# Three activation tiles on the ScalarE queue and a reordered head, in an S5 + SwiGLU kernel

## The chip, the cores and the metric

One core of a Trainium2 chip runs the kernel. TensorE (PE) multiplies matrices and transposes, VectorE (DVE), ScalarE (ACT) and GpSimd (POOL) do the elementwise work, and SyncE (SP), ACT and POOL issue DMAs. The metric is the device time of one execution in microseconds, and of several executions the median.

## The reference

`x` is 2048 x 512 in bf16. It is layer-normalised without weights, and the result `xn` goes through two branches whose outputs are added to `x`:

```
xn = (x - mean) / sqrt(var + 1e-5)
A: Bu = xn @ B_bar^T (complex);  h_t = Lam_bar * h_{t-1} + Bu_t;  y = 2 Re(h @ C^T) + xn * Dskip
B: (silu(xn @ w_gate) * (xn @ w_up)) @ w_down          512 -> 1376 -> 512
out = x + A + B
```

## The kernel before

The 2048 rows are 16 tiles of 128 rows, in four chunks of four tiles (512 rows). For each chunk there are three kinds of matmul stage: gate and up (`gateup_tile`, line 427, 11 column tiles of 128), the B projection of the state space branch (`bproj_tile`, line 352), and the output (`out_ffn` line 514, `out_ssm` line 524). DVE runs the scans and rotations, ACT evicts PSUM. Instructions run on each engine in the order in which the program text issues them. DVE's longer work is put on a list (`queue`) and taken off it between matmul stages by estimated costs (`pump`, `need`); nothing of the change is on that list.

The change lies in the head, which makes the first chunk ready while the weights still arrive. What there is to know of it:

- **Loads** (lines 120 to 146). SP issues `x` tile 0, the two halves of gate's first column group (`load_w1_half`, line 118; a half is two of the four slices of 128 rows of the weight, 192 KB), `x` tile 2, the two halves of up's first group, `x` tile 3, then gate's and up's second group (line 113), the four `x` tiles of chunk 1 in one DMA (line 136), and the transposing loads of B (line 139). ACT issues `x` tile 1, then loads its function table (line 123). A tile of `x` is 128 KB.
- **Layernorm of one tile.** `ln_stats` (DVE, lines 183 and 184: statistics into `mv`), `ln_rstd_act` (ACT, lines 194 and 195: Ln and Exp give `rstd`), `norm_dve` (DVE, line 207: writes `xn`), `xT_pe` (PE, line 219: four 128 x 128 transposes into PSUM), and the copy of PSUM to `xnT` (ACT, line 223; for tile 3 DVE, line 221).
- **Matmuls** (`head_mm(i, groups, k0, k1)`, line 609): for tile `i` and the first three column tiles, a matmul of 128 x 128 x 128 for each slice k from k0 to k1. They need `xnT` of tile i and the weight's slices.
- **Dummy matmuls** (`dummy`, line 581) ahead of the first transpose, on a tile of zeros: ten of 512 columns, and three of 128 columns between the two halves of tile 0.

The order of the head is the text at lines 613 to 656:

```
dummy(10, CW)
... statistics, rstd and norm of tiles 0 and 1, transposes of tile 0
head_mm(0, wg_g, 0, HK)
xT_pe(1)
head_mm(0, wu_g, 0, HK)
ln_stats(2); ln_rstd_act(2)
head_mm(0, wg_g, HK, KD)
head_mm(0, wu_g, HK, KD)
ln_stats(3); norm_dve(2); ln_rstd_act(3)
head_mm(1, wg_g); xT_pe(2); norm_dve(3)
head_mm(1, wu_g); prm_transpose(); head_mm(2, wg_g)
xT_pe(3, on_dve=True); head_mm(2, wu_g)
```

After them come the matmuls of tile 3, the evictions of the held banks, and the steady stages.

Of the kernel before, what the change touches and what calls it, by code (L numbers as in the profile page):

```python
# [23 lines left out]
def kernel(  # L24
# [17 lines left out]
    nc = tc.nc  # L42
# [4 lines left out]
    CW = 512  # L47
# [3 lines left out]
    TPC = CW // 128  # L51
# [22 lines left out]
    def bank(shape=(128, CW), dtype=F32):  # L74
        return psum.tile(list(shape), dtype, name="ps")
# [4 lines left out]
    x_v = A_x[0].rearrange("(n p) d -> p n d", p=128)  # L80
# [5 lines left out]
    xall = const.tile([128, NT, D], BF16, name="xall")  # L86
# [3 lines left out]
    wg_g, wu_g = [], []  # L90
# [14 lines left out]
    def wslice(groups, fi, k):  # L105
        for (a, b), t in zip(fgroups, groups):
            if a <= fi < b:
                return t[:, k, (fi - a) * 128:(fi - a) * 128 + fsz[fi]]


    def load_w1(q, tiles, view, gi):
        a, b = fgroups[gi]
        q.dma_start(out=tiles[gi][:], in_=view[:, :, a * 128:min(F, b * 128)])


    def load_w1_half(tiles, view, gi, k0, k1):
        a, b = fgroups[gi]
        nc.sync.dma_start(out=tiles[gi][:, k0:k1, :], in_=view[:, k0:k1, a * 128:min(F, b * 128)])  # L118

    nc.sync.dma_start(out=xall[:, 0, :], in_=x_v[:, 0, :])  # L120
    nc.vector.memset(xall[:, 1, 0:2], 0.0)
    nc.scalar.dma_start(out=xall[:, 1, :], in_=x_v[:, 1, :])
    nc.scalar.preload_act_table_set("natural_log_exp_and_others")
    load_w1_half(wg_g, wg_v, 0, 0, KD // 2)
    load_w1_half(wg_g, wg_v, 0, KD // 2, KD)
    nc.sync.dma_start(out=xall[:, 2, :], in_=x_v[:, 2, :])  # L126
    load_w1_half(wu_g, wu_v, 0, 0, KD // 2)
    load_w1_half(wu_g, wu_v, 0, KD // 2, KD)
    nc.sync.dma_start(out=xall[:, 3, :], in_=x_v[:, 3, :])
    load_w1(nc.sync, wg_g, wg_v, 1)  # L130
    load_w1(nc.sync, wu_g, wu_v, 1)
    prm_rows = const.tile([128, 128], BF16, name="prm_rows")
# [44 lines left out]
    def xn_tile(c):  # L177
        if c not in xn_c:
            xn_c[c] = lnp.tile([128, TPC, D], BF16, name="xn")
        return xn_c[c]  # L180

    def ln_stats(n):
        nc.vector.bn_stats(out=stats[:, n, 0, :], in_=xall[:, n, :])  # L183
        nc.vector.bn_aggr(out=mv[:, n, :], in_=stats[:, n, 0, :])
# [8 lines left out]
    def ln_rstd_act(n):  # L193
        nc.scalar.activation(out=lnv[:, n:n + 1], in_=mv[:, n, 1:2], func=ACT.Ln, bias=eps_t[:])
        nc.scalar.activation(out=rstd[:, n:n + 1], in_=lnv[:, n:n + 1], func=ACT.Exp, scale=-0.5)
# [9 lines left out]
    def norm_dve(n, lo=0, hi=D):  # L205
        c, i = divmod(n, TPC)
        nc.vector.tensor_scalar(out=xn_tile(c)[:, i, lo:hi], in0=xall[:, n, lo:hi], scalar1=mv[:, n, 0:1],  # L207
                                scalar2=rstd[:, n:n + 1], op0=ALU.subtract, op1=ALU.mult)
# [6 lines left out]
    def xT_pe(n, k0=0, k1=KD, on_dve=False):  # L215
        c, i = divmod(n, TPC)
        tp = bank((128, KD, 128), BF16)
        for k in range(k0, k1):
            nc.tensor.transpose(out=tp[:, k, :], in_=xn_tile(c)[:, i, k * 128:(k + 1) * 128], identity=ident[:])  # L219
        if on_dve:  # L220
            nc.vector.tensor_copy(out=xnT[:, k0:k1, n * 128:(n + 1) * 128], in_=tp[:, k0:k1, :])
        else:
            nc.scalar.copy(out=xnT[:, k0:k1, n * 128:(n + 1) * 128], in_=tp[:, k0:k1, :])
# [355 lines left out]
    def dummy(n, cols):  # L579
        for _ in range(n):  # L580
            nc.tensor.matmul(warm[:, 0:cols], lhsT=junk[:, 0:128], rhs=junk[:, 0:cols], start=True, stop=True)
# [21 lines left out]
    def head_mm(i, groups, k0=0, k1=KD, tiles=range(H)):  # L603
        which = 0 if groups is wg_g else 1
        for fi in tiles:
            if len(held) <= fi:
                held.append((bank(), bank()))
            for k in range(k0, k1):
                nc.tensor.matmul(held[fi][which][:, i * 128:(i + 1) * 128], lhsT=wslice(groups, fi, k),  # L609
                                 rhs=xnT[:, k, i * 128:(i + 1) * 128], start=(k == 0), stop=(k == KD - 1))  # L610

    HK = KD // 2
    dummy(10, CW)
    ln_stats(0)
    ln_rstd_act(0)
    ln_stats(1)
# [6 lines left out]
    norm_dve(1)  # L623
    head_mm(0, wg_g, 0, HK)
    xT_pe(1)
    head_mm(0, wu_g, 0, HK)
    ln_stats(2)
    ln_rstd_act(2)
    head_mm(0, wg_g, HK, KD)
    head_mm(0, wu_g, HK, KD)  # L630
    ln_stats(3)
    norm_dve(2)
    ln_rstd_act(3)
    head_mm(1, wg_g)
    xT_pe(2)
# [148 lines left out]
```

## Time and profile before

| What | Value |
|---|---|
| median of 3 runs | 181.02 us (180.7 to 181.13) |
| the profiled execution's own time | 181.21 us |
| its span, first to last instruction | 179.4 us |
| mean granted TensorE clock | 0.999 |
| busy PE / DVE / ACT / POOL | 97% / 86% / 58% / 13% |
| DMA, mean over the span | 87 GB/s |
| the chain that ended last | PE 93%, DMA 2%, SP's issues 1%, DVE 1% |

The chain of waits is followed back from the last instruction to what released it. In the timeline, a row is start, duration, engine, line, operation, output and inputs; several like instructions are merged into one row with their count, and a bracket tells how long the engine had stood idle and what ended it. Times are microseconds from the span's start. PEld is TensorE's weight load, SPq and ACTq the issuing of DMAs. Matmuls are pipelined: a 128-column one is shown at about 0.22 us, while the next starts 0.06 us after it.

### The profile page before, as it was taken

The page shows a single profiled execution, that of the slowest core. Times are in us where ns is not written, and L with a number is a line of the kernel's source. Part 1 is how long each engine was busy: PE and PEld are TensorE (multiplying, and loading weights), DVE is VectorE, ACT ScalarE, POOL GpSimd, SP SyncE. Part 2 cuts the span into 40 slices and gives each one's busy share as a digit, 9 for nine tenths or more (in the row PEclk, how much of TensorE's full clock was granted, in tenths as well). Part 3 has the DMA queues.
Part 4 walks back from the last instruction along what each step waited for, and adds up shares of the span by engine and source line. Part 5 has one row for each costly group of instructions (what it writes and reads, how often), then busy time and mean ns, then how long its engine had stood idle before and what let it go on. Part 6 is the DMA issues. An engine that isn't in the chain of part 4 may idle for free.

```text
span 179.4 us, 2491 instructions
## 1 busy us (share of the span) xinstructions
PE 173.4 (97%) x908; PEld 83.4 (46%) x924; DVE 155.0 (86%) x248; ACT 104.8 (58%) x190; POOL 23.4 (13%) x30
## 2 busy tenths in 40 slices
PE   7899999999999999999999999999999999999993
PEld 2684444443444444444444444444444444444742
DVE  3649998799999999999999999999999986996033
ACT  3459956998299959022799661024866949805000
POOL 7001100000500000025400000014000004315000
PEclk9999999999999999999999999999999999999999
DMA  5999757994036600011840000007300007964512
GB/s 147 294 263 210 163 98 177 357 190 109 5 72 168 252 4 0 0 11 22 112 93 2 0 0 4 0 0 80 37 0 5 0 0 109 139 103 45 76 58 61
DMA packets 28492, 15.53 MB, mean 87 GB/s; under 512 B 18336, under 2 KB 28416, under 8 KB 28448
## 3 DMA queue, kind: packets, MB, share of 16 engines
q1 hardware_dynamic: 24592, 11.87, 28.5%
q0 software_dynamic: 3456, 3.28, 14.4%
q10 hardware_dynamic: 432, 0.23, 0.4%
q8 instruction: 7, 0.11, 0.3%
q14 instruction: 5, 0.04, 0.1%
HBM read 8.03 MB, written 5.24 MB: 74 GB/s over the span
## 4 chain that ended last, share of the span: by engine, by line
PE 93%; DMA 2%; SPq 1%; DVE 1%; issue 1%
PE ps L427 36%; PE ps L514 21%; PE ps L352 15%; PE ps L524 15%; DMA xall<-in_A_x_dram 2%; PE ps L609 2%; PE ps L453 2%; PE ps L463 1%; SPq L118 1%; DVE stats L183 0%; PE ps L219 0%; SPq L126 0%; SPq L120 0%; DVE xn L207 0%; DVE xall L527 0%
## 5 line engine op out<-in xcount | busy, mean ns | idle before, releaser
L514 PE MATMUL ps<-wd_sb,guT 128*128 128x512 bf16 (+4 forms) x195 | 38.6, 355 | 0.2
L427 PE MATMUL ps<-xnT,wg 128*128 128x512 bf16 x143 | 37.6, 379 | 0.3
L427 PE MATMUL ps<-xnT,wu 128*128 128x512 bf16 x146 | 37.5, 379 | 0.1
L394 DVE TENSOR_TENSOR_SCAN g<-r_t,car,u 128x512 bf16<-128x512 f32 x24 | 28.9, 1263 | 0.0
L524 PE MATMUL ps<-CF,wt 128*128 128x512 bf16 (+2 forms) x140 | 28.1, 355 | 0.2
L352 PE MATMUL ps<-xnT,BT 128*128 128x512 bf16 x126 | 28.2, 379 | 0.1
L514 PEld LDWEIGHTS <-guT 128*128 128x128 bf16 (+1 forms) x198 | 18.5, 98 | 19.9
L441 ACT ACTIVATE guT<-ps 128x512 bf16<-128x512 f32 x40 | 25.2, 629 | 2.5 <-PE ps L427 2.3
L442 ACT CAST u<-ps 128x512 bf16<-128x512 f32 x40 | 24.7, 618 | 2.7 <-PE ps L427 2.7
L427 PEld LDWEIGHTS <-wu 128*128 128x128 bf16 x148 | 14.5, 98 | 17.5
L427 PEld LDWEIGHTS <-wg 128*128 128x128 bf16 x148 | 14.3, 98 | 17.6 <-issue 0.8
L530 ACT CAST res<-ps 128x512 bf16<-128x512 f32 x12 | 6.8, 582 | 23.5 <-PE ps L524 23.5
L524 PEld LDWEIGHTS <-wt 128*128 128x128 bf16 x144 | 13.4, 98 | 14.3
L531 POOL DMA_DIRECT2D out_dram<-res x12 | 10.5, 1033 | 72.6 <-ACT res L530 67.5
L352 PEld LDWEIGHTS <-BT 128*128 128x128 bf16 x128 | 12.5, 98 | 15.1
L354 ACT CAST u<-ps 128x512 bf16<-128x512 f32 x32 | 17.7, 614 | 2.4 <-PE ps L352 2.2
L486 ACT ACTIVATE xr<-xall,nb,rstd 128x512 bf16<-128x512 bf16 x16 | 12.0, 808 | 8.4 <-DVE xall L492 5.9
L183 DVE BATCH_NORM_STATS2 stats<-xall 128x6 f32<-128x512 bf16 x16 | 10.7, 671 | 3.2 <-DMA xall<-in_A_x_dram 3.2
L446 DVE TENSOR_TENSOR guT<-guT,u 128x1024 bf16<-128x1024 bf16 x20 | 13.5, 679 | 0.0
L527 DVE TENSOR_TENSOR xall<-ps,xall 128x512 bf16<-128x512 f32 (+2 forms) x6 | 3.1, 514 | 9.1 <-PE ps L524 9.1
L199 POOL TENSOR_TENSOR rstd<-ve,neg_half 128x4 f32<-128x4 f32 x3 | 5.3, 1751 | 43.6 <-DVE ve L198 43.6
L362 DVE TENSOR_TENSOR pm<-u,c 128x2048 bf16<-128x2048 bf16 x8 | 9.8, 1221 | 1.2 <-ACT c L279 1.1
(101 smaller groups left out, 169.0 us busy)
## 6 DMA issues: line engine op xcount, KB each, us to landing
out_dram<-in_A_x_dram SPq DMA_DIRECT2D x1, 1536.0 KB, 8.7
out_dram<-res POOLq DMA_DIRECT2D x12, 128.0 KB, 3.2
out_dram<-xall POOLq DMA_DIRECT2D x3, 512.0 KB, 5.7
wd_sb<-in_B_w_down_dram SPq DMA_DIRECT2D x1, 1280.0 KB, 10.1
xall<-in_A_x_dram SPq DMA_DIRECT2D x1, 1024.0 KB, 5.9
wg<-in_B_w_gate_dram SPq DMA_DIRECT2D x1, 512.0 KB, 6.1
wu<-in_B_w_up_dram SPq DMA_DIRECT2D x1, 512.0 KB, 7.1
xall<-in_A_x_dram SPq DMA_DIRECT2D x1, 512.0 KB, 7.9
```

Of the source, the lines that this page charges most:

```text
L183: nc.vector.bn_stats(out=stats[:, n, 0, :], in_=xall[:, n, :])
L352: nc.tensor.matmul(ps[:], lhsT=BT[:, part, k, q * 128:(q + 1) * 128], rhs=xnT[:, k, c * CW:(c + 1) * CW], start=(k == 0), stop=(k == KD - 1))
L354: nc.scalar.copy(out=u_tiles[c][:, part, q, :], in_=ps[:])
L394: V.tensor_tensor_scan(out=g()[:, part, q, :], data0=r_t[:, q:q + 1].to_broadcast([128, CW]), data1=u_tiles[c][:, part, q, :], initial=ini ...
L427: nc.tensor.matmul(ps[:fs, lo:hi], lhsT=wslice(groups, fi, k), rhs=xnT[:, k, c * CW + lo:c * CW + hi], start=(k == 0), stop=(k == KD - 1))
L441: nc.scalar.activation(out=guT[:fs, fi, :], in_=psg[:fs], func=ACT.Silu)
L442: nc.scalar.copy(out=u_pair[c][:fs, fi % 2, :], in_=psu[:fs])
L446: products.append(lambda: V.tensor_tensor(out=g, in0=g, in1=u, op=ALU.mult))
L486: nc.scalar.activation(out=box["xr"][:], in_=xall[:, n, :], func=ACT.Identity, scale=rstd[:, n:n + 1], bias=nb[:, n:n + 1])
L514: nc.tensor.matmul(o[:], lhsT=gu_tiles[c][:fsz[fi], fi, i * 128:(i + 1) * 128], rhs=wd_sb[:fsz[fi], fi, lo:hi], start=(fi == 0), stop=False)
L524: nc.tensor.matmul(o[:], lhsT=w_tiles[c][:, part, q, i * 128:(i + 1) * 128], rhs=CF[:, part, q, lo:hi], start=False, stop=(part == 1 and q ...
L531: nc.gpsimd.dma_start(out=out_v[:, n, lo:hi], in_=res[:, lo:hi], accum_op=ALU.add)
```

## The change

The loads of `x` tiles 2 and 3 leave SP's queue and go on ACT's, behind tile 1 and ahead of ACT's table load. One of the ten dummy matmuls goes. In the head's order, gate's second half comes ahead of up's first half, and the normalisation of tile 2 comes ahead of tile 3's statistics on DVE. The instructions are otherwise the same on every engine.

```diff
     nc.sync.dma_start(out=xall[:, 0, :], in_=x_v[:, 0, :])
     nc.vector.memset(xall[:, 1, 0:2], 0.0)
-    nc.scalar.dma_start(out=xall[:, 1, :], in_=x_v[:, 1, :])
+    for n in range(1, TPC):
+        nc.scalar.dma_start(out=xall[:, n, :], in_=x_v[:, n, :])
     nc.scalar.preload_act_table_set("natural_log_exp_and_others")
     load_w1_half(wg_g, wg_v, 0, 0, KD // 2)
     load_w1_half(wg_g, wg_v, 0, KD // 2, KD)
-    nc.sync.dma_start(out=xall[:, 2, :], in_=x_v[:, 2, :])
     load_w1_half(wu_g, wu_v, 0, 0, KD // 2)
     load_w1_half(wu_g, wu_v, 0, KD // 2, KD)
-    nc.sync.dma_start(out=xall[:, 3, :], in_=x_v[:, 3, :])
     load_w1(nc.sync, wg_g, wg_v, 1)
...
-    dummy(10, CW)
+    dummy(9, CW)
...
     head_mm(0, wg_g, 0, HK)
     xT_pe(1)
-    head_mm(0, wu_g, 0, HK)
     ln_stats(2)
     ln_rstd_act(2)
     head_mm(0, wg_g, HK, KD)
+    norm_dve(2)
+    head_mm(0, wu_g, 0, HK)
     head_mm(0, wu_g, HK, KD)
     ln_stats(3)
-    norm_dve(2)
     ln_rstd_act(3)
     head_mm(1, wg_g)
     xT_pe(2)
```

## The prediction

> **What bounds the kernel now.** I read the page first, then the chain of waits in order of time, then the timeline of the head engine by engine, then the DMA rows. The page's chain gives the engine:
>
> ```profile
> PE 93%; DMA 2%; SPq 1%; DVE 1%; issue 1%
> ```
>
> PE sets the end almost everywhere. The chain in order of time shows where it does not:
>
> ```profile
> 3.68 4.33 DMA xall<-in_A_x_dram
> 8.04 0.70 DVE stats L183
> 8.77 0.18 DVE mv L184
> 8.95 0.31 DVE xn L207
> 9.31 0.40 PE ps L219 x4
> 9.71 0.67 PE ps L609 x12
> ```
>
> Up to 9.31 us the chain runs through the load of `x` tile 3, its statistics, and the normalisation of tile 2, which stands behind those statistics on DVE. From 9.31 on it is PE to within 3 us of the end, with no gap over 0.1 us except where matmul records are missing. So what the change can win or lose is where PE stands when it leaves the head; every 0.1 us there is 0.1 us at the end, unless something later was ready only just in time. The head on PE (timeline):
>
> ```profile
> 5.25 0.28 PE L219 MATMUL ps<-ident,xn 128*128 128x128 bf16 x2
> 5.99 0.50 PE L609 MATMUL ps<-xnT,wg 128*128 128x128 bf16 x6 [0.18 <-ACT xnT L223]
> 6.32 0.39 PE L219 MATMUL ps<-ident,xn 128*128 128x128 bf16 x4
> 6.83 0.51 PE L609 MATMUL ps<-xnT,wu 128*128 128x128 bf16 x6
> 7.18 0.50 PE L609 MATMUL ps<-xnT,wg 128*128 128x128 bf16 x6
> 7.51 0.50 PE L609 MATMUL ps<-xnT,wu 128*128 128x128 bf16 x6
> 7.85 0.83 PE L609 MATMUL ps<-xnT,wg 128*128 128x128 bf16 x12
> 9.31 0.40 PE L219 MATMUL ps<-ident,xn 128*128 128x128 bf16 x4 [0.63 <-DVE xn L207]
> 10.38 0.83 PE L609 MATMUL ps<-xnT,wg 128*128 128x128 bf16 x12
> ```
>
> A group of six takes 0.33 us of PE (6.83 was held until up's first half landed), twelve take 0.67, four transposes 0.22. The hole before 9.31 is the largest. Then ACT, which turns each tile's variance into `rstd` and copies the transposes out:
>
> ```profile
> 6.74 0.58 ACT L223 COPY xnT<-ps 128x512 bf16<-128x512 bf16 x1 [0.53 <-PE ps L219]
> 7.22 0.30 ACT L194 ACTIVATE lnv<-mv,eps_t 128x1 f32<-128x1 f32 x1
> 7.55 0.20 ACT L195 ACTIVATE rstd<-lnv 128x1 f32<-128x1 f32 x1
> 8.99 0.29 ACT L194 ACTIVATE lnv<-mv,eps_t 128x1 f32<-128x1 f32 x1 [1.23 <-DVE mv L184]
> 9.31 0.20 ACT L195 ACTIVATE rstd<-lnv 128x1 f32<-128x1 f32 x1
> 9.74 0.58 ACT L223 COPY xnT<-ps 128x512 bf16<-128x512 bf16 x1 [0.23 <-PE ps L219]
> ```
>
> The copy at 9.74 is tile 2's; it stands behind tile 3's Ln and Exp in ACT's order, and gate's matmuls of tile 2 (10.38) start as it ends. Last, the DMA rates (columns after the label: busy of PE, DVE, ACT, POOL and so on, clock, DMA share, GB/s):
>
> ```profile
> 2.20:3.00 0.80, 0.80 (x4) 0.25 (x3) 0.00 (x0) 0.40 (x1) 0.80 (x2) 1.00 1.03 345
> 3.30:5.60 2.30, 2.30 (x13) 1.05 (x12) 2.12 (x7) 1.03 (x5) 0.82 (x2) 1.00 0.89 205
> 5.60:8.00 2.40, 2.09 (x35) 1.80 (x33) 1.03 (x3) 1.60 (x5) 0.00 (x0) 1.00 1.01 306
> ```
>
> The DMA engines are loaded (share 0.89 to 1.03) from 2.2 us to past 8.0. By issue plus time to landing, tile 0 lands at 3.0, tile 1 at 3.4, gate's halves at 3.9 and 5.9, tile 2 at 6.3, up's halves at 6.8 and 7.4, tile 3 at 8.0.
>
> **The change part by part.**
>
> *Issues.* ACT gains two DMA issues of 0.38 us (tile 1's row) ahead of its table load, which moves from 1.31 to 2.08 and ends at 3.36 (1.28 long). The first Ln runs at 3.98, so 0.62 us of cover hide it; without that cover the 0.77 us would delay every tile. SP loses two issues of 0.47: up's halves are issued 0.5 earlier, gate's and up's second group, the 512 KB of `x` and the B transposes up to 1.0 earlier. B is first read at 20.19 us and the B issues end long before (the first four at 13.17, the others at 20.1), so I cost the later ones at nothing. Were that cover gone, PE would wait at 20.19. By the program's list of waits, each of SP's later issues waits for the DMA eight places ahead of it (the 512 KB of `x` for gate's first half, the first B load for tile 2): these land before the old issue times 5.22 and 5.90, so nothing behind them gets later. POOL's queue is unchanged.
>
> *Arrivals.* Tiles 2 and 3 are issued at 1.3 and 1.7. Tile 2 lands between 3.8 (2.5 after issue, as tile 1) and 5.6 (4.3, the slowest row of the 128 KB loads), tile 3 between 4.2 and 6.0. The bytes are the same 1.31 MB, and SP's weights now share the engines with 256 KB more of `x` that used to stand behind or between them. Gate's second half, which ended the first 0.66 MB, now ends about 0.92 MB, and lands between 5.9 and 6.8 (6.8 is the old landing of the load that ended 0.98 MB). Up's second half is now the last: between 7.4 (its old time) and 8.0 (tile 3's time, the old end of the same 1.31 MB). Below 7.4 it could go if two queues keep the 345 GB/s of the first row, where both were active, through the stretch that carried 205 with one; above 8.0 if the interleaving costs the weight packets more than their share, for which no row speaks, so I allow 8.8, as far above 8.0 as gate's second half may slip. I take 7.8, close to the row of the same bytes.
> [...]
>
> *The dummy.* Dummies start 0.43 us apart up to 4.61; the tenth starts at 5.04 and the first transpose follows it at 5.25, so it costs 0.21 us. Tile 0's first half is written at 4.98 (4.66 plus 0.32), so the transposes can start at 5.04. The chain behind moves with it: transposes of the second half 5.53 to 5.32 (input written by 5.3), ACT's copies 5.56 to 5.35 (ACT is free at 5.30), gate's first six 5.99 to 5.78, tile 1's transposes 6.32 to 6.11 (its norm ends at 5.75), tile 1's copy 6.74 to 6.53, ending 7.11. That is 0.21 us won here, if the clock holds (a rival below); bounds 0 and 0.21.
>
> *Tile 2's chain.* Statistics start when tile 1's norm ends, 5.77 instead of 6.27; `mv` is there at 6.68. Ln waits on ACT for tile 1's copy: 7.08 instead of 7.22 (the next ACT instruction starts some 0.1 before the end of the one ahead, as between the two copies at 5.56). Exp 0.33 later, 7.41; norm 0.24 after that (9.31 to 9.55 for tile 3), 7.65, done at 8.05. In before it ended at 9.25. So PE's hole before 9.31 is gone as far as tile 2's norm goes: 1.2 us earlier.
>
> *Tile 3's chain.* Its statistics now stand behind a norm that waits for ACT. They start at 7.96 instead of 8.04: the landing two us earlier buys 0.08. `mv` and Ln follow at the old distances (0.95): 8.91, Exp 9.23, done 9.43. Behind it on ACT stands tile 2's copy, which can therefore not start before 9.35 to 9.43. It was at 9.74. This limits the whole gain to 0.31 to 0.39, whatever the DMAs do; I take 0.35. Tile 3's norm starts at 9.47 (9.55 before), ahead of its transposes, which PE reaches at 10.7 at the earliest.
>
> *PE's order.* Gate's second six at 6.33 or its landing (up to 6.8), up's six and six to 7.8 + 0.05 + 0.33 = 8.18, tile 1's gate 0.67 to 8.85, tile 2's transposes there: 0.46 before 9.31. With the landing as a variable L, transposes start at L + 1.05, and the gain is 8.26 - L. Which half of gate or up runs first costs PE nothing in itself: the same 24 matmuls.
>
> *Sum.* The smaller of 0.46 (weights) and 0.35 (ACT's order) is 0.35 us, carried by an unbroken PE to the end. From there to the span's end the terms do not change. The profiled execution would go from 181.21 (span 179.4 and 1.8 around it) to 180.86; it stands 0.19 above the median, so the forecast is 181.02 - 0.35 = 180.67 us.
>
> **The rivals.**
>
> *The weights come late (slower).* Up's second half lands at 8.8 because tiles 1 to 3 take their share of packets ahead of it. For it: the engines are full, and gate's second half spread to 4.2 us from issue. Against it: the bytes ahead grow by 128 KB only, 0.43 us at 306 GB/s. The gain is 8.26 - L, so it decides from L = 8.26; at 8.8 PE leaves 0.54 later: 181.56.
>
> *The transfer is hidden anyway.* L at 8.2, no change: 181.0. The two queues then cost what the order wins.
>
> *The clock.* The dummies run at 0.43 us for 512 columns and the tenth at 0.21: the clock opened at about 5.0, 3.8 us after the first matmul, and the removed one started just then. If it opens later when PE is less dense, the 47 matmuls and transposes between 5.04 and 8.85 take 0.11 instead of 0.06 each: up to 2.4 us on PE, of which the waits hide about half; 181.5 to 182.5. Against it: all that PE did before 5.04 is unchanged.
> [...]
>
> **How the numbers follow.** The median's three runs lie 0.24% apart, so 0.3% (0.54 us) is about what can be told from no change. The forecast has 0.72: gain 0.25 to 0.45 by its terms, with some 0.2 for the spread of medians and for terms read off a single execution; I give 0.39 to within 0.3% and 0.33 to beyond it. Late weights 0.15 (0.12 slower, 0.03 within), hidden anyway 0.07 (within), clock 0.06 (0.05 slower, 0.01 within). Together faster 0.33, same 0.50, slower 0.17. The range: down to 180.1 (the 0.46 and the 0.43 between the fastest and slowest run shown), up to 181.5, which takes in most of late weights and leaves out the clock. The forecast's own range is 180.3 to 180.95.
>
> **What would show it.** In the profile after: ten rows become nine and the transposes start at 5.04; tile 2's statistics start at 5.77 without a wait on a DMA; its norm near 7.65; the wait "DVE stats on DMA xall" falls from 3.2 us over 3 to 1.9 over 1; tile 2's transposes near 8.85 with no wait on DVE; tile 2's copy right behind tile 3's Exp near 9.4; gate's matmuls of tile 2 near 10.0. New waits of PE's weight load on wg and wu should show before 8.0. The prediction is wrong if up's second half lands after 8.3, if 512-column dummies are followed by slow transposes, or if PE shows a hole after 10 us that was not there.

## The result and the profile after

The changed kernel takes 181.5 us (median of 20 runs, 181.06 to 181.96) against 180.9 us of the kernel before on the same chip (20 runs, 180.52 to 181.48): a ratio of 1.003 with a 95% interval of 1.002 to 1.0041. It is slower by 0.54 us (0.36 to 0.74); forecast was 180.67, 0.35 us faster. The profiled execution went from a span of 179.4 to one of 180.1 us (it took 181.92 us, 0.42 more than the median). The page's chain after:

```profile
PE 51%; DVE 36%; ACT 8%; issue 3%; DVEq 0%
```

Before, PE was 93% of it. Now the chain leaves PE at 90.87 us, and ahead of that it runs mostly through DVE, so that DVE's lateness reaches the end. Three stretches carry the 0.7 us between the two spans. Elsewhere PE runs at a constant distance to before: +0.17 or 0.18 us from 13 us on, +0.50 from 90.9 us to the end.

**The head.** ACT's timeline after (start, duration, engine, line, operation, output and inputs; the bracket is the idle time ahead and what ended it):

```profile
7.18 0.59 ACT L222 COPY xnT<-ps 128x512 bf16<-128x512 bf16 x1 [0.78 <-PE ps L218]
7.67 0.30 ACT L193 ACTIVATE lnv<-mv,eps_t 128x1 f32<-128x1 f32 x1
9.50 0.29 ACT L193 ACTIVATE lnv<-mv,eps_t 128x1 f32<-128x1 f32 x1 [1.30 <-DVE mv L183]
9.82 0.20 ACT L194 ACTIVATE rstd<-lnv 128x1 f32<-128x1 f32 x1
9.93 0.57 ACT L222 COPY xnT<-ps 128x512 bf16<-128x512 bf16 x1
```

The last row is tile 2's copy: behind tile 3's Ln and Exp, as forecast, but at 9.93 instead of 9.35 to 9.43. The whole chain is 0.5 to 0.6 late because tile 1's copy is (7.18; 6.53 was forecast). PE's timeline after shows why:

```profile
5.92 0.80 PE L608 MATMUL ps<-xnT,wg 128*128 128x128 bf16 x6
...
10.55 0.83 PE L608 MATMUL ps<-xnT,wg 128*128 128x128 bf16 x12 [0.60 <-ACT xnT L222]
...
13.46 0.81 PE L426 MATMUL ps<-xnT,wg 128*128 128x512 bf16 x2
```

The first six gate matmuls are spread over 0.80 us instead of 0.50. In this execution the record of TensorE's granted clock opens (begins, with 1.0) at 7.08 us, against 5.02 before. Between 5.98 and 7.04 matmuls of 128 columns start 0.10 to 0.11 us apart, and from 7.12 on 0.06 in a group; in before the dummies start 0.43 us apart up to the tenth at 5.04, and the next matmul starts 0.21 behind that one. The first matmul of 512 columns, the end of the head, is at 13.46, 0.18 later than the 13.28 of before.

**The place near 29 us.** DVE's timeline, after and then before:

```profile
28.46 0.69 DVE L271 TENSOR_SCALAR pm<-pm 128x1024 f32<-128x1024 f32 x1
29.67 0.69 DVE L273 TENSOR_SCALAR pm<-pm 128x1024 f32<-128x1024 f32 x1 [0.51 <-ACT s L278]
```

```profile
28.27 0.69 DVE L272 TENSOR_SCALAR pm<-pm 128x1024 f32<-128x1024 f32 x1
29.07 0.69 DVE L274 TENSOR_SCALAR pm<-pm 128x1024 f32<-128x1024 f32 x1
```

The second operation started 0.80 us behind the first, and now 1.21. The bracket blames ACT's write of `s`, and it misleads: in before that ACT operation ran from 28.27 to 29.33, so the DVE operation, at 29.07, did not wait for its end, and after it ended at 29.52, 0.15 us before the start. DVE is 0.60 late from here on. At 86 us that reaches ACT and at 90 us PE, which had gone on at +0.18. PE after, then before:

```profile
89.68 1.03 PE L426 MATMUL ps<-xnT,wu 128*128 128x512 bf16 x4
90.87 0.81 PE L426 MATMUL ps<-xnT,wg 128*128 128x512 bf16 x3 [0.16 <-ACT guT L440]
```

```profile
89.50 1.03 PE L427 MATMUL ps<-xnT,wu 128*128 128x512 bf16 x4
90.36 1.03 PE L427 MATMUL ps<-xnT,wg 128*128 128x512 bf16 x4
```

1.19 us from group to group instead of 0.86: 0.33 us lost, and not won back. In between, ACT's normalisation of chunk 3 had slipped from 86.14 to 86.77, and its evictions behind it.

**The closing.** DVE's last operation, after and then before:

```profile
176.92 0.29 DVE L526 TENSOR_TENSOR xall<-ps,xall 128x128 bf16<-128x128 f32 x1 [0.15 <-PE ps L523]
```

```profile
176.42 0.29 DVE L527 TENSOR_TENSOR xall<-ps,xall 128x128 bf16<-128x128 f32 x1 [0.15 <-PE ps L524]
```

It is 0.50 late, but the span is 0.69 longer (180.125 against 179.433). From this operation's start to the last instruction's it is 3.14 us after and 2.95 before. Here and in the table below, "last instruction" is SP's last record. The sum for the two profiled executions is 0.18 (head) + 0.33 (DVE's stall) + 0.19 (closing) = 0.70.

### The profile page after: what moved, and what is told of

It reads as the page before. It is cut to its first block, busy times and chain, and to the rows that moved or that the text cites. A ratio compares the mean times of both kernels' runs of the same rounds, so it can differ in the third digit from the quotient of the medians.

```text
span 180.1 us, 2490 instructions
## 1 busy us (share of the span) xinstructions
PE 174.0 (97%) x907; PEld 84.1 (47%) x923; DVE 155.1 (86%) x248; ACT 104.7 (58%) x190; POOL 23.4 (13%) x30
## 3 DMA queue, kind: packets, MB, share of 16 engines
HBM read 8.03 MB, written 5.24 MB: 74 GB/s over the span
## 4 chain that ended last, share of the span: by engine, by line
PE 51%; DVE 36%; ACT 8%; issue 3%; DVEq 0%
PE ps L513 16%; PE ps L426 15%; PE ps L523 11%; DVE pm L361 8%; DVE g L393 7%; DVE stats L182 4%; PE ps L351 4%; DVE guT L445 3%; PE ps L580 2%; DVE pm L274 2%; ACT u L353 2%; DVE u L375 1%; DVE mv L183 1%; DVE CF L337 1%; DVE u L371 1%
## 5 line engine op out<-in xcount | busy, mean ns | idle before, releaser
L445 DVE TENSOR_TENSOR guT<-guT,u 128x1024 bf16<-128x1024 bf16 x20 | 13.5, 680 | 0.0
```

The source lines that it names most:

```text
L445: products.append(lambda: V.tensor_tensor(out=g, in0=g, in1=u, op=ALU.mult))
```

## The experiments

In the table, "head" is the start of the first matmul of 512 columns, "stall" says whether DVE stops for 0.44 to 0.46 us ahead of the operation near 29 us, and "closing" is the time from the start of DVE's last operation to that of the last instruction. Kernels of one group ran on one chip, where the kernel before had medians of 180.9, 180.93, 180.8, 180.84, 180.9 and 181.14 us (groups 0 to 5).

| Group | Kernel | median, us | ratio to before, 95% | head | stall | closing |
|---|---|---|---|---|---|---|
| 0 | before (shown first) | 180.9 | 1 | 13.28 | no | 2.95 |
| 0 | the change | 181.5 | 1.003 [1.002, 1.0041] | 13.46 | yes | 3.14 |
| 1 | after_d10 | 181.6 | 1.0039 [1.0025, 1.0053] | 13.15 | yes | 3.14 |
| 1 | after_pad | 181.09 | 1.0006 [0.9996, 1.0015] | 13.02 | no | 3.14 |
| 1 | before_pad | 181.26 | 1.0021 [1.0007, 1.0035] | 13.07 | yes | 2.95 |
| 1 | before_d9 | 181.14 | 1.0009 [0.9995, 1.0022] | 13.87 | no | 2.96 |
| 2 | after_d10_pad | 181.32 | 1.0022 [1.0009, 1.0035] | 13.09 | no | 3.14 |
| 2 | loads_only | 180.71 | 0.9995 [0.9984, 1.0005] | 12.37 | no | 3.14 |
| 2 | no_norm_d10 | 180.74 | 0.9992 [0.9982, 1.0002] | 12.59 | no | 3.14 |
| 2 | norm_pad | 181.25 | 1.0021 [1.0009, 1.0033] | 13.28 | no | 2.95 |
| 3 | before_look2 | 180.62 (one run) | | 12.69 | no | 2.96 |
| 3 | before_look3 | 181.37 (one run) | | 13.43 | no | 2.95 |
| 3 | before_pad2 | 180.97 | 0.9996 [0.9979, 1.0013] | 13.26 | no | 2.95 |
| 3 | no_norm | 180.45 | 0.9972 [0.9957, 0.9986] | 12.23 | no | 3.15 |
| 4 | after_again | 181.37 | 1.0022 [1.0004, 1.0039] | 12.95 | yes | 3.15 |
| 4 | after_pad_b | 181.13 | 1.0016 [1.0002, 1.0029] | 12.99 | no | 3.14 |
| 4 | no_norm_b | 180.5 | 0.9981 [0.9967, 0.9994] | 12.46 | no | 3.14 |
| 4 | no_norm_pad | 181.01 | 1.0002 [0.9989, 1.0016] | 12.87 | yes | 3.13 |
| 5 | no_norm_s8 | 180.28 | 0.9957 [0.994, 0.9974] | 12.55 | no | 2.61 |
| 5 | before_s8 | 180.82 | 0.9986 [0.9973, 0.9999] | 13.20 | no | 2.62 |

### Dummy or DVE's program: the first four

The theories were the late clock (the tenth dummy is what opens it) and a stall that depends on how many instructions DVE has ahead. "Pad" is one more small memset on DVE at the start, which nothing reads:

```diff
 nc.vector.memset(eps_t[:], EPS)
+pad_t = const.tile([128, 1], F32, name="pad_t")
+nc.vector.memset(pad_t[:], 0.0)
```

and d10 and d9 change the number of dummies:

```diff
-dummy(9, CW)      # after_d10, on the changed kernel; before_d9 is the reverse on before
+dummy(10, CW)
```

> The changed kernel with the tenth dummy matmul put back. If the missing dummy keeps TensorE's clock from opening at 5.0 us (it opened near 7.1 in the changed kernel's profile), the clock opens near 5.0 here, tile 2's copy stands near 9.5 and the time falls by about 0.3 us below the changed kernel, 181.2 or less. If the moment of opening is chance and has nothing to do with the dummy, the time stays at 181.5 or rises by up to 0.2 (the dummy's own time). In both cases the DVE stall of 0.46 us near 29.2 us should stay.

Measured 181.6: no fall. The clock opened at 5.3 us and the head came 0.31 earlier than in the first trace of the changed kernel, but the stall and the loss at 90 us were there. The tenth dummy is not what the change loses.

> The changed kernel with one more DVE memset of one column, in DVE's idle time before 3 us: it moves every later DVE instruction on by one place in DVE's program and costs no time of its own. If the DVE stall of 0.46 us near 29.2 us hangs on the place of that instruction in DVE's program, it goes, DVE is 0.4 earlier from there on, PE does not wait at 90.9 and the time falls by 0.3 to 0.4, to about 181.15. If it is caused by the order of work or by DMA traffic, it stays, and the time stays at 181.5.

Measured 181.09, still with nine dummies. DVE's timeline:

```profile
28.02 0.69 DVE L273 TENSOR_SCALAR pm<-pm 128x1024 f32<-128x1024 f32 x1
28.83 0.69 DVE L275 TENSOR_SCALAR pm<-pm 128x1024 f32<-128x1024 f32 x1
```

0.81 us apart again, and on PE the same two groups are at 89.23 and 90.10. An added instruction takes the stall away.

> The kernel before with the same extra DVE memset before 3 us. Its DVE program then stands at the same places as the changed kernel's from tile 3 on. If the place matters, the stall of about 0.46 us near 29 us appears here too and the time rises by 0.3 to 0.5, to about 181.3, although the order of work and the DMAs are those of the kernel before. If not, the time stays at 180.9.

Measured 181.26, slower than before by 0.38 us (0.13 to 0.63), with the stall in the old kernel:

```profile
28.08 0.69 DVE L274 TENSOR_SCALAR pm<-pm 128x1024 f32<-128x1024 f32 x1
29.30 0.69 DVE L276 TENSOR_SCALAR pm<-pm 128x1024 f32<-128x1024 f32 x1 [0.52 <-ACT s L281]
```

A memset that nothing reads makes DVE stop 28 us later, with the same wrong name in the bracket. So it is the place in the program, and not anything that the change computes.

> The kernel before with nine dummy matmuls for ten. If the missing dummy delays the clock, the time rises by 0.2 to 0.5. If the clock's moment is chance, the time stays or falls by up to 0.1: tile 1 is ready sooner, but tile 3's load at 8.0 still holds tile 2 back.

Measured 181.14, 0.21 above before and inside the interval. Its trace has the latest head of all (13.87), with tile 3's statistics and the clock (7.1 us) both late.

### The parts of the change

loads_only is the loads' part alone on before:

```diff
-    nc.scalar.dma_start(out=xall[:, 1, :], in_=x_v[:, 1, :])
+    for n in range(1, TPC):
+        nc.scalar.dma_start(out=xall[:, n, :], in_=x_v[:, n, :])
...
-    nc.sync.dma_start(out=xall[:, 2, :], in_=x_v[:, 2, :])
...
-    nc.sync.dma_start(out=xall[:, 3, :], in_=x_v[:, 3, :])
```

no_norm is the change without the DVE move, and no_norm_d10 the same with ten dummies:

```diff
-    norm_dve(2)          # in the changed kernel, ahead of up's first half
...
     ln_stats(3)
+    norm_dve(2)          # back to where before has it
     ln_rstd_act(3)
```

norm_pad is before with the pad and the DVE move alone:

```diff
+    norm_dve(2)
     ln_stats(3)
-    norm_dve(2)
     ln_rstd_act(3)
```

after_d10_pad is the changed kernel with ten dummies and the pad.

> The changed kernel with the tenth dummy back and the extra DVE memset, so loads and order alone are left of the change. If the DVE stall was the whole loss and the head wins what was forecast less the dummy, the time is 0.15 to 0.35 below the kernel before, 180.6 to 180.8. If the order on DVE (tile 2's norm ahead of tile 3's statistics) spends what the loads win, it is within 0.1 of the kernel before, 180.85 to 181.05.

Measured 181.32, above what was expected: without the stall and with the tenth dummy it still loses 0.4 us (0.16 to 0.63) to before. Something else costs too.

> The kernel before with only the loads of tiles 2 and 3 on ScalarE's queue; DVE's program keeps its places, so no stall near 29 us. Tile 3's statistics follow tile 2's at once, tile 2's norm comes by about 8.0 and tile 3's Ln and Exp stand before 8.5, so ACT does not hold tile 2's copy back: PE leaves the head 0.2 to 0.5 earlier, 180.4 to 180.75. If the weights coming late takes it back, PE waits for up's second half past 8.2 and the time is 180.9 or more.

Measured 180.71, 0.09 us below before and inside the interval, where 0.05 to 0.4 below was expected. Its trace has a head (12.37) 0.91 earlier than the first trace of before, of which 0.72 was left at the span's end. That execution took 180.48, 0.23 less than the kernel's median, so the trace shows more gain than the median does.

> The kernel before with the loads moved and gate's second half ahead of up's first, but tile 2's norm behind tile 3's statistics as before and ten dummies. As the loads alone, and PE does not wait for up's first half with gate's second at hand: 180.4 to 180.7, at or up to 0.1 below the loads alone. If the order of the halves counts for nothing, equal to the loads alone.

Measured 180.74, also within the interval (0.9982 to 1.0002). The order of gate's and up's halves adds nothing that can be told.

> The kernel before with only tile 2's norm moved ahead of tile 3's statistics, and the extra DVE memset that moves DVE's program past the stall. Tile 2's transposes no longer wait for tile 3's load and come near 8.55, but tile 3's Ln and Exp stay where they were and tile 2's copy stands behind them on ACT: gain 0 to 0.25, 180.65 to 180.95. If the norm in front delays tile 3's chain, the time rises by 0.1 to 0.3.

Measured 181.25, by the ratio a loss of 0.38 us (0.16 to 0.6) where 0.1 to 0.3 was expected, with no stall. Tile 3's load landed early here, at 7.52, and did not help: its statistics start at 8.38, behind tile 2's norm, which waited for ACT.

### What an execution of before looks like

> The kernel before, unchanged, a second look with a profile. If its first profile was a late execution (tile 3's load landed at 8.0 us, 181.21 for a median of 180.9), tile 3's statistics start clearly earlier here, near 7.0 to 7.6, tile 2's copy on ACT near 9.2 to 9.4, first 512-column matmul near 12.8 to 13.0, span near 179.0. If the first profile was typical, these stand at 8.0, 9.74 and 13.28 again.

> A third look at the kernel before. As the second: tile 3's statistics near 7.0 to 7.6 if the first profile was late, near 8.0 if it was typical.

No edit: two more executions of before. DVE's timeline of the first of them:

```profile
7.44 0.70 DVE L183 BATCH_NORM_STATS2 stats<-xall 128x6 f32<-128x512 bf16 x1 [0.47 <-DMA xall<-in_A_x_dram]
```

and of the second:

```profile
8.19 0.69 DVE L183 BATCH_NORM_STATS2 stats<-xall 128x6 f32<-128x512 bf16 x1 [0.47 <-DMA xall<-in_A_x_dram]
```

Tile 3's statistics start when it lands, at 7.44, 8.04 (the execution that the prediction was read from) and 8.19, and the first 512-column matmul follows at 12.69, 13.28 and 13.43, 5.24 or 5.25 later each time. The executions took 180.62, 181.21 and 181.37 us. So in these three the landing passes one to one into the time. The execution that the forecast was read from took 0.3 more than the median of 180.9; that tile 3 lands earlier in a median execution fits this, but is not shown by itself.

> The kernel before with two extra DVE memsets before 3 us for the one of the earlier run. If the stall near 29 us hangs on one place in DVE's program, two more places on there is none, and the time is that of the kernel before, within 0.15. If any extra DVE instruction costs the 0.33 us of the earlier run, the time is again 0.3 or more above.

The pad with its memset twice, so two places more:

```diff
+nc.vector.memset(pad_t[:], 0.0)
```

Measured 180.97, as before; no stall. One place more has it, two places more do not. It is not "a longer program is slower".

> The changed kernel without the move of tile 2's norm: loads, halves' order and nine dummies. With no stall and tile 3's chain not held back it should be below the kernel before: the 0.05 to 0.1 of loads and order, and 0.1 to 0.2 of the dummy, so 0.15 to 0.3 below, 180.5 to 180.7. If the dummy counts for nothing, it is equal to the run with ten (0.06 below the kernel before).

Measured 180.45, faster than before by 0.5 us (0.25 to 0.78), more than expected. DVE's timeline, and ACT's:

```profile
6.66 0.66 DVE L182 BATCH_NORM_STATS2 stats<-xall 128x6 f32<-128x512 bf16 x1
7.36 0.18 DVE L183 BATCH_NORM_AGGREGATE mv<-stats 128x2 f32<-128x6 f32 x1
7.79 0.83 DVE L206 TENSOR_SCALAR xn<-xall,mv,rstd 128x512 bf16<-128x512 bf16 x2 [0.25 <-ACT rstd L194]
```

```profile
7.66 0.28 ACT L193 ACTIVATE lnv<-mv,eps_t 128x1 f32<-128x1 f32 x1
...
8.69 0.58 ACT L222 COPY xnT<-ps 128x512 bf16<-128x512 bf16 x1 [0.52 <-PE ps L218]
```

Tile 3's statistics fit into the time in which tile 2's `rstd` is being made, and tile 2's norm (the first of the two at 7.79) is not late for it. ACT has Ln and Exp of tile 3 done before tile 2's copy, which starts at 8.69 as PE delivers it. With the norm in front, tile 3's statistics wait for ACT and ACT's copy then waits for them. after_pad, the changed kernel without the stall and with the clock open at 4.0 us, shows that chain undisturbed (ACT's timeline):

```profile
8.97 0.29 ACT L195 ACTIVATE lnv<-mv,eps_t 128x1 f32<-128x1 f32 x1 [1.30 <-DVE mv L185]
9.30 0.20 ACT L196 ACTIVATE rstd<-lnv 128x1 f32<-128x1 f32 x1
9.47 0.59 ACT L224 COPY xnT<-ps 128x512 bf16<-128x512 bf16 x1
```

### Order and stall apart, on one chip

after_again, after_pad_b and no_norm_b are repeats; no_norm_pad is no_norm with the pad, which gives DVE one place more and so the stall.

> The changed kernel again: order moved, stall present. 0.5 to 0.6 above the kernel before, as measured. First 512-column matmul of the steady stages at 13.0 to 13.5 us, PE waits about 0.33 near 90.9.

> The changed kernel with one extra DVE memset: order moved, no stall. 0.3 to 0.45 below the changed kernel on this chip if the stall is worth what PE loses at 90.9; equal to it if the first comparison was between chips.

> Loads, halves' order and nine dummies, norm behind the statistics as before: order not moved, no stall. 0.4 to 0.7 below the changed kernel with the memset if the order on DVE is the larger cause (head's end 12.2 to 12.6 against 13.0 to 13.5); within 0.2 of it if the stall was nearly all.

> As the last, with one extra DVE memset: order not moved, stall present. 0.3 to 0.45 above the last if the two causes add; less if PE, ahead of DVE by the earlier head, has no slack or more slack at 90.9.

Medians, in us:

| | no stall | stall |
|---|---|---|
| norm of tile 2 not moved | 180.5 (no_norm_b) | 181.01 (no_norm_pad) |
| norm of tile 2 ahead | 181.13 (after_pad_b) | 181.37 (after_again) |

Moving the norm costs 0.63 without the stall and 0.36 with it; the stall costs 0.51 and 0.24, and in the traces 0.29 to 0.35. Both are outside the 0.3 to 0.45 expected, one above and one below; after_again came out 0.47 above before (0.5 to 0.6 expected, head at 12.95 for 13.0 to 13.5), no_norm_b as expected. The half-widths of the single ratios are 0.2 to 0.3 us, so the two pairs do not differ for certain, and the trace's 0.33 lies within both. Moving the norm does both things: it puts tile 3 late, and, since it waits for two semaphores where it now stands, it brings one more wait instruction, so that the operation near 29 us becomes DVE's 64th, behind a short wait.

### The closing

The column "closing" left 0.19 us open: all kernels so far with tiles 2 and 3 on ACT's queue have 3.13 to 3.15, all others 2.95 or 2.96. The rows of the timeline leave out waits and drains; the trace's records with them, numbered from each engine's first, show the following (start in us):

```
DVE  before     62nd 29.00 wait 0.02     63rd 29.07 op 0.69      64th 29.80 op
     after      63rd 29.20 wait 0.02     64th 29.67 op
     after_pad  63rd 28.02 op 0.69       64th 28.76 wait 0.02    65th 28.83 op
SP   before     79th 178.00 wait   80th 178.50 wait, last store   81st 178.59 drain   82nd 178.67 drain
     after      78th 178.69 wait, last store   79th 178.77 drain  80th 179.25 drain
```

On DVE the 64th starts 0.44 to 0.46 us behind the end of a wait of 0.02 us, and 0.03 to 0.04 behind the end of an operation of 0.69 us, which is long enough to hide a gap of 0.46. On SP the 80th starts 0.46 to 0.47 us behind the end of the one ahead. In before that is the wait for the last store, which lands at 178.18, so that the first 0.15 us of the 0.47 pass before the landing and 0.32 after it; the change takes two DMAs out of SP's program, the 80th becomes a drain that stands behind that wait, and none of the 0.47 falls ahead of the landing. The rival was that ACT's longer queue makes the closing longer. To tell them apart, SP's program was made eight instructions longer (POOL's by three) by cutting one copy of `x` to `out`, which SP issues near 56 us, into nine, on no_norm and on before:

```diff
-    nc.sync.dma_start(out=out[0, 0:(NT - TPC) * 128, :], in_=A_x[0, 0:(NT - TPC) * 128, :])
+    for lo, hi in [(n, n + 1) for n in range(8)] + [(8, NT - TPC)]:
+        nc.sync.dma_start(out=out[0, lo * 128:hi * 128, :], in_=A_x[0, lo * 128:hi * 128, :])
```

> The full reference is computed; the one copy of x to out that SyncE issues near 56 us is split by rows into nine copies of the same bytes, so SyncE's program has eight instructions more. In all 18 kernels traced so far SyncE's 80th recorded instruction starts 0.47 to 0.50 us behind the one ahead of it; with the loads on SyncE this is the wait for the last store, which must wait for most of that time anyway, with tiles 2 and 3 on ScalarE's queue it is the second drain behind that wait, where nothing hides it (from the last DVE operation's start to the last instruction's 2.95 us against 3.14). Theory of the place: the 80th is now among the closing waits for semaphores that are long met, ahead of the wait for the last store, and is hidden behind that store's landing; the last stretch falls from 3.15 to about 2.75 us and the median from 180.45 to about 180.05. Rival, two more loads on ScalarE's queue make the closing longer by themselves: 3.15 stays, median 180.35 to 180.6.

> The full reference is computed; the kernel before with the same split of the copy, eight more instructions on SyncE. Theory of the place: the wait for the last store is no longer the 80th and ends with the landing, 1.77 instead of 2.08 us after the last DVE operation's start; the last stretch falls from 2.95 to about 2.65 us, the median by 0.3 to about 180.6, so that moved and unmoved loads differ by 0.1 in the closing instead of 0.19. Rival (queue): 2.95 stays, median as before within 0.15.

The closing fell to 2.61 and 2.62 us, somewhat below the 2.75 and 2.65 expected, and the same in both kernels whichever queue loads `x`. In no_norm_s8 the records are:

```
SP   no_norm_s8 79th 176.45 wait   80th 176.95 wait   ...   86th 177.46 wait, last store   87th 177.53 drain   88th 177.59 drain
```

The 80th is again 0.50 behind the 79th, now among waits that were met long before the last store lands. The last store lands at 177.44, the wait for it starts at 177.46, and the drains follow 0.07 us apart. From the last store's landing to SP's last record it is 1.19 us in before, 1.39 in the change, and 0.86 and 0.85 in the two kernels with the split. The theory of the queue falls. In time, before_s8 is 0.0014 of 181.14 below before, 0.25 us (0.02 to 0.49), where 0.3 was expected; no_norm_s8 is 0.0043, or 0.78 us (0.47 to 1.09) below it, and the fastest of all. Against no_norm (0.9972 on another chip) that is about 0.27, where the closing gives 0.54; its traced head was 0.32 later than no_norm's, and the intervals are wider than the difference.

## Why the prediction was wrong, point by point

- *Sum* ("From there to the span's end the terms do not change", an "unbroken PE to the end"): this step failed, twice. Beyond the head lie 0.33 us from DVE's stall and 0.19 us more from SP's in the closing. The traces of before show nothing of the first: there the 64th stands 0.03 us behind an operation of 0.69 us. Of the second they have a part, as a wait for the last store that goes on for 0.32 us after the landing; before_s8 is rid of it, and the change pays more. Together 0.52, against a measured loss of 0.54, which leaves nothing won in the head.
- *Issues* counted SP's two issues as 0.47 us each that other loads gain. That they also leave SP's program two instructions shorter was not thought of; that is the 0.19. The account of the change calls the instructions otherwise the same on every engine; counted with the waits they are not: DVE has 271 recorded for 270, SP 83 for 85, ACT 234 for 232. The cover of ACT's table load held (2.28 to 3.56, first Ln at 4.02).
- *Sum* again, the size of the head's gain: the forecast was made against one execution, in which tile 3 landed at 8.0 us, and took the whole 0.35 off the median. Over all traces the head is at 13.26 us on average with the loads and the order of before (seven traces, 12.69 to 13.87) and at 13.11 with those of the change (six, 12.95 to 13.46): 0.15 us won instead of 0.35. Those seven executions took on average 0.26 us more than their kernels' medians, the six 0.05 more. If that time was lost in the head, as it was in the three executions of before, the heads of median executions would be at 13.00 and 13.06, and nothing would be won; this is an estimate from these averages. In the seven traces tile 3's statistics start at 8.01 on average, so the landing read was not a late one among the traced.
- *Tile 3's chain* was right in mechanism and size: statistics 7.96, Ln 8.91 and copy 9.35 to 9.43 forecast; 8.04, 8.97 and 9.47 in after_pad. What it showed was not drawn out: it is the move itself that makes the cap. Left where it was, with the loads moved, tile 2's copy is at 8.69 in no_norm (to 9.33 in no_norm_pad) and the head at 12.51 on average (six traces, 12.23 to 12.87), 0.6 earlier than with the move. The prediction compared the new order with the old kernel, and not with the new loads in the old order.
- *PE's order* was right: tile 2's transposes start at 8.84 (8.85 forecast). A hole on PE after 10 us, named as a sign of being wrong, did appear: 0.60 us ahead of 10.55, where PE waits for ACT's late copy, and 0.16 us ahead of 90.87.
- *Arrivals* was right for the weights: gate's second half landed at 6.71 (5.9 to 6.8 forecast), up's second half at 7.78 (7.8). It was wrong for tile 3, which landed at 6.90 (4.2 to 6.0 forecast) and at 5.50 to 7.10 in the twelve traces with the moved loads; with tile 2's norm ahead of its statistics this cost nothing. What the second queue buys is the sequence: tile 3 is there 1.1 us earlier in the first pair of traces, and on average at 6.17 us against 7.93 in the eight with the old loads. The rivals of late weights and of the hidden transfer did not come about. The last of the same bytes is issued 1.0 us earlier (2.68 for 3.68) and lands on average 0.6 us earlier (7.32 against 7.93).
- *The dummy*: with nine the transposes start at 5.04 to 5.26 us (5.17 on average, nine traces; 5.04 forecast), with ten at 5.19 to 5.47 (5.36, eleven traces), so most of the 0.21 is won there. What it is worth in time is not shown: three pairs, each on different chips, are lower with nine (181.09 against 181.32, 180.45 against 180.74, 181.5 against 181.6), and before_d9 is 0.21 above before on the same chip, within its interval.
- *The clock* as a rival: the late opening came in the first trace of the changed kernel (7.08 us) and cost some tenths of the head there, but not as the rival had it. The records open between 3.96 and 6.95 us with ten dummies (5.5 on average, eleven traces) and between 4.01 and 7.1 with nine (5.6, eight traces), in kernels whose PE does the same work up to 5.04 us. So the moment differs from run to run, where the prediction had only one; what sets it is not shown. The traces show no delay by the missing dummy, but eight and eleven traces that scatter over 3 us would not show one of a few tenths.

## What to carry to other kernels

When instructions are moved between engines, count what it does to the number of instructions that each engine has, waits included: here one more on DVE and two fewer on SP cost 0.33 and 0.19 us far from the edit, and moving the count on, by one memset on DVE or eight DMA issues on SP, got each part back, the closing's with more. Look at an execution of the kernel before more than once: a forecast made against one execution carries what that execution lost by chance. And where a change has several parts, compare each with the other parts in place; here the new loads with nine dummies and the halves' order, but without the move on DVE, are 0.34 to 0.5 us faster than before, and the move takes that away. The loads alone, and the loads and halves' order with ten dummies, are not told from before.

## What the runs showed of the hardware

- **A stall by place.** In all 20 traces SP's 80th recorded instruction starts 0.46 to 0.47 us after the end of the one ahead of it, and in the five with a short wait as DVE's 63rd (the change, after_d10, after_again, before_pad, no_norm_pad) DVE's 64th starts 0.44 to 0.46 us late; in the other 15 the 63rd is an operation of 0.69 us and the gap is 0.03 to 0.04. The profile puts the DVE stall down to an ACT write that ended 0.15 us earlier. What happens at that place is not shown. The DMA rows (queue, kind, packets, MB, share of 16 engines) of the trace after, from 27 to 31 us and from 179.5 to 180.2 us, are:

```profile
q1 hardware_dynamic: 1367, 0.69, 71.0%
```

```profile
q14 instruction: 1, 0.01, 4.7%
```

Around DVE's stall the queue that the profile calls "instruction" moves nothing. Behind SP's it moves one packet of 8 KB: in all 20 traces such a packet starts 0.61 to 0.88 us after the start of SP's 80th instruction, so that this one cannot have waited for it, and in the two kernels with eight more instructions on SP it comes earlier together with the 80th. The times of this queue's packets go with DVE's count too, though none falls at the stall: one of q14 starts at 20.0 to 20.4 us in the five traces in which DVE has 272 recorded instructions, and at 32.1 to 34.1 in the fifteen with 270 or 271.
- **The landing of the same load differs from execution to execution:** tile 3 lets its statistics start at 7.44, 8.04 and 8.19 us in three executions of the same kernel, and each difference is found again in the execution's time.
- **The clock's opening differs** from 3.96 to 7.1 us, 2.7 to 5.9 us behind the first matmul at 1.23 (19 traces; one has no record of it).
